# A fused attention and two-layer MoE kernel on one core: product 3 earlier in the second matmul, the next slice's x made later and for both halves at once, weight conversion in one half of the stage, and GpSimd's queue in emission order

## The chip, the cores and the metric

The kernel runs on one core of a Trainium2 chip (trn2). The metric is the device time of one execution in microseconds; lower is better. Engines are called by the names of the profile: PE (TensorE), PEld (its weight loads), DVE (VectorE), ACT (ScalarE), POOL (GpSimd) and SP (SyncE, which here only issues DMAs).

## What is computed

```python
def _attn_ref(q, k, v, g_norm):            # q, k, v: (8, 8, 576, 64)
    kv = np.einsum('bhsd,bhse->bhde', k, v)
    out = np.einsum('bhsd,bhde->bhse', q, kv)
    rms = np.sqrt(np.mean(out * out, axis=-1, keepdims=True) + 1e-06)
    return out / rms * g_norm

x = attn_out.transpose(0, 2, 1, 3).reshape(4608, 512)
h = x @ moe_w_in                           # 512 x 2048
x = (h / (1 + np.exp(-1.702 * h))) @ moe_w_out
h = x @ moe2_w_in
return (h - np.tanh(h)) @ moe2_w_out       # 4608 x 512
```

The weights arrive as 64-bit numbers and are converted on the chip.

## The kernel before

**Stages.** The 4608 tokens are cut into 8 slices of 576 (one batch each), and there are two layers, so the program runs 16 stages (l, n): layer l = 0 for n = 0 to 7, then layer l = 1. A stage has two halves. M1 (`m1`) multiplies x by the first weight matrix and applies the nonlinearity on ACT (L717); its results stand in the tiles `gt`. M2 (`m2`) multiplies these by the second weight matrix. The first slices use special code (`m1_plain`, `m2_plain`, `front_early`, `back_early`).

**Seven products.** Both halves replace the 8 block products of a 2 by 2 block multiplication by 7, numbered 1 to 7, whose operands are sums and differences of blocks. Each operand is split into a high and a low fp16 part, and three matmuls (high by high, high by low, low by high) stand for one in fp32. M2 takes its products in the order `ORDER2`, four steps each, 28 steps in all, 12 matmuls a step. A product accumulates in one pair of PSUM banks, X, Y or Z, halves d = 0 and d = 1. Products 1, 6, 7 and 4 share X, and each goes on adding to what the ones before left there, so PE may not start one before ACT has read the sum out (`scaled`, L839). What belongs to Y or Z is then added on DVE (`fma`, L833).

**The operands of M2.** For step i, DVE may first subtract one block of `gt` from another (`jA`, L771), ACT writes the high part (`jB`, L785) and DVE the low part (`jC`, L791) into one of seven buffers `jt`. The weights of M2 are streamed on SP's queue: 14 blocks `st` of 512 KB (`stream`, L812) through a ring of 4 buffers, one block for two steps. The weights of M1 stay on the chip (`wi`, 8 tiles).

**What runs beside.** Generators that are stepped at the end of every step (`tick`), at a rate for M1 and one for M2 (`add_side`), emit the side work. In stages (0, 2) to (0, 6) these are:

- `front(n + 1)` in M1: head products and numerators of the attention of the next slice. Its inputs come on POOL's queue, four units of keys and values of 640 KB (`xo<-atp`, L388) and two parts of queries of 576 KB (`scratch<-atp`, L388). It ends with the inverse roots, which are written to DRAM (`rd<-scratch`, L540).
- `back(n + 1)` in M2: the roots are read back, broadcast (`scratch<-rd`, L552, four of 288 KB), multiplied into the numerators (L653), and the seven operands of x are made by DVE subtractions (L344), ACT (L354) and DVE (L357). It ends with the fetch of the first inputs of the slice after.
- `conv1`: the second layer's 64-bit weights are loaded into `cbk` (L148, L149), turned into fp32 and split into fp16 by ACT and DVE (`words`, L160 to L166, and L175 to L181, L231), and written back to DRAM (`wid<-cbk`, L236; `wod<-cbk`, L239). All these DMAs are on POOL's queue.

In stage (0, 7) the first layer's `wi` are replaced by the second layer's: 8 reloads `wi<-wid` of 896 KB (L664) on POOL's queue. In layer 1 the side work is only loading x of the next slice (`scratch<-x2d`, L380, on SP's queue) and splitting it.

**What sets the order.** On PE and SP the instructions stand as they are emitted:

```python
man.enter_context(tc.manual_schedule(engines=frozenset([ENG.PE, ENG.SP])))
```

On the other engines a scheduler puts them in order from its own estimate of times. All engines run their own lists in order.

## Time and profile before

| | us |
|---|---|
| median of 3 runs | 1499.76 (1498.02 to 1500.09) |
| the profiled execution | 1500.06 |
| its span | 1498.3 |
| PE busy | 1431.6 (96%) |
| DVE busy | 1170.0 (78%) |
| ACT busy | 881.6 (59%) |
| POOL busy | 153.2 (10%) |
| DMA moved | 247.57 MB |

The profiled execution took 1.8 us more than its span, which runs from its first to its last instruction, and 0.3 us more than the median of the runs. A busy share is a mean over the stages, so the rows below are taken stage by stage.

### The profile page before, as it was taken

Reading aid. Unit: us, or ns where it says so; the run is one execution under the profiler, and the core shown is the slowest. Engines: PE = TensorE matmul, PEld = TensorE weight load, DVE = VectorE, ACT = ScalarE, POOL = GpSimd, SP = SyncE. Lnnn points to the kernel's source line nnn. Section 1 sums busy time; section 2 is a strip of 40 time slices with the busy share of each in tenths; the row PEclk is TensorE's granted clock in tenths of the full one; section 3 lists DMA queues with packets and bytes.
Section 4 is the critical chain, followed back from the end, with each engine's and each line's share of the span. In section 5 each row is a group of like instructions: output and inputs, shape, how many; then the busy total and the mean of one; then the engine's idle time right before and its main releaser. Section 6 shows DMA issues by size and latency. Waiting matters only on the chain.

```text
span 1498.3 us, 30084 instructions
## 1 busy us (share of the span) xinstructions
PE 1431.6 (96%) x11922; PEld 1108.8 (74%) x11922; DVE 1170.0 (78%) x2267; ACT 881.6 (59%) x1918; POOL 153.2 (10%) x238
## 2 busy tenths in 40 slices
PE   7999988999999899899989999999999999999998
PEld 5667756667777676677767777777777777777776
DVE  4998889587895776868879887868777787878485
ACT  5775554655756557567566555656464655555463
POOL 0001010121111202213031000000000000000000
PEclk9999999999999999999999999999999999999999
DMA  8776837267284582763788435160705243331504
GB/s 293 229 224 198 253 104 235 99 214 241 91 298 154 169 291 81 224 221 109 233 284 291 139 106 164 59 194 16 221 34 190 72 139 107 105 125 61 169 15 159
DMA packets 104686, 247.57 MB, mean 165 GB/s; under 512 B 10624, under 2 KB 55296, under 8 KB 104544
## 3 DMA queue, kind: packets, MB, share of 16 engines
q1 hardware_dynamic: 83504, 161.49, 33.4%
q0 software_dynamic: 21040, 84.15, 17.7%
q8 instruction: 93, 1.52, 0.4%
q14 instruction: 49, 0.40, 0.1%
HBM read 202.62 MB, written 42.98 MB: 164 GB/s over the span
## 4 chain that ended last, share of the span: by engine, by line
PE 71%; DVE 12%; DMA 8%; issue 5%; ACT 4%; SPq 0%; POOL 0%; DVEq 0%; POOLq 0%; ACTq 0%
PE X L896 7%; PE X L898 7%; PE X L897 7%; PE X L710 6%; PE X L712 6%; PE X L711 6%; PE Y L896 4%; PE Y L898 4%; PE Y L897 3%; DMA st<-wod 3%; PE Z L710 3%; PE Z L712 3%; PE Z L711 3%; DVE jt L791 2%; PE Z L896 2%
## 5 line engine op out<-in xcount | busy, mean ns | idle before, releaser
L785 ACT ACTIVATE jt<-gt 128x576 f16<-128x576 f32 x420 | 284.4, 682 | 180.3 <-PE X L898 63.8
L791 DVE SCALAR_TENSOR_TENSOR jt<-gt,jt 128x576 f16<-128x576 f32 x420 | 312.6, 754 | 74.7 <-ACT jt L785 71.3
L896 PE MATMUL X<-jt,st 128*128 128x288 f16 x960 | 274.5, 286 | 4.5 <-ACT gt L938 1.7
L897 PE MATMUL X<-jt,st 128*128 128x288 f16 x960 | 274.5, 286 | 2.9 <-DVE jt L791 2.9
L898 PE MATMUL X<-jt,st 128*128 128x288 f16 x960 | 274.5, 286 | 0.0
L710 PE MATMUL X<-xo,wi 128*128 128x288 f16 x896 | 256.4, 286 | 8.0 <-ACT mscratch L743 8.0
L712 PE MATMUL X<-xo,wi 128*128 128x288 f16 x896 | 256.2, 286 | 0.0
L711 PE MATMUL X<-xo,wi 128*128 128x288 f16 x896 | 256.2, 286 | 0.0
L896 PEld LDWEIGHTS <-st 128*128 128x128 f16 x1680 | 165.3, 98 | 64.3 <-DMA st<-wod 21.9
L898 PEld LDWEIGHTS <-st 128*128 128x128 f16 x1680 | 165.3, 98 | 49.4 <-issue 7.0
L897 PEld LDWEIGHTS <-st 128*128 128x128 f16 x1680 | 165.2, 98 | 49.0 <-issue 6.7
L710 PEld LDWEIGHTS <-wi 128*128 128x128 f16 x1568 | 153.3, 98 | 52.2 <-issue 13.4
L711 PEld LDWEIGHTS <-wi 128*128 128x128 f16 x1568 | 153.4, 98 | 48.6 <-issue 10.8
L712 PEld LDWEIGHTS <-wi 128*128 128x128 f16 x1568 | 153.4, 98 | 38.7
L771 DVE TENSOR_TENSOR gt<-gt 128x576 f32<-128x576 f32 x240 | 176.7, 751 | 1.6 <-ACT gt L717 1.2
L743 ACT COPY mscratch<-X 128x288 f32<-128x288 f32 x336 | 133.3, 397 | 75.5 <-PE X L712 69.1
L748 DVE TENSOR_TENSOR mscratch<-Z,mscratch 128x288 f32<-128x288 f32 x224 | 101.7, 454 | 75.1 <-PE Z L712 40.7
L896 PE MATMUL Y<-jt,st 128*128 128x288 f16 x480 | 137.3, 286 | 2.0 <-ACT gt L938 1.3
L897 PE MATMUL Y<-jt,st 128*128 128x288 f16 x480 | 137.3, 286 | 0.4 <-DVE jt L791 0.4
L898 PE MATMUL Y<-jt,st 128*128 128x288 f16 x480 | 137.3, 286 | 0.0
L710 PE MATMUL Z<-xo,wi 128*128 128x288 f16 x448 | 128.3, 286 | 0.4 <-DVE mscratch L748 0.4
L712 PE MATMUL Z<-xo,wi 128*128 128x288 f16 x448 | 128.1, 286 | 0.0
(249 smaller groups left out, 2505.2 us busy)
## 6 DMA issues: line engine op xcount, KB each, us to landing
st<-wod SPq DMA_DIRECT2D x210, 512.0 KB, 4.6
xo<-atp POOLq DMA_DIRECT2D x20, 640.0 KB, 6.2
scratch<-x2d SPq DMA_DIRECT2D x32, 288.0 KB, 6.0
cbk<-w_in POOLq DMA_DIRECT2D x32, 256.0 KB, 3.4
cbk<-w_out POOLq DMA_DIRECT2D x32, 256.0 KB, 5.0
scratch<-atp POOLq DMA_DIRECT2D x14, 576.0 KB, 6.3
scratch<-rd POOLq DMA_DIRECT2D x28, 288.0 KB, 8.8
x2d<-mscratch SPq DMA_DIRECT2D x28, 288.0 KB, 5.0
```

What stands on the lines that cost most here:

```text
L710: nc.tensor.matmul(out=out, lhsT=wh, rhs=xh, start=fresh and kt == 0, stop=False, skip_group_check=k)
L711: nc.tensor.matmul(out=out, lhsT=wh, rhs=xl, start=False, stop=False, skip_group_check=k)
L712: nc.tensor.matmul(out=out, lhsT=wl, rhs=xh, start=False, stop=kt == 1, skip_group_check=k)
L743: main(nc.scalar.copy(out=b.ap, in_=x))
L748: main(nc.vector.tensor_tensor(out=b.ap, in0=add[0], in1=b.ap, op=ALU.add))
L771: tt = lambda o, a, b: main(nc.vector.tensor_tensor(out=G[:, :, o, :], in0=G[:, :, a, :], in1=G[:, :, b, :], op=ALU.subtract))
L785: main(nc.scalar.activation(out=j[:, :, 0, :], in_=GT[STEPS2[i][1]][:, :, QD[STEPS2[i][0]], :], func=AF.Copy, scale=SX))
L791: main(nc.vector.scalar_tensor_tensor(out=j[:, :, 1, :], in0=GT[STEPS2[i][1]][:, :, QD[STEPS2[i][0]], :], scalar=SX, in1=j[:, :, 0, :], op ...
L896: nc.tensor.matmul(out=out, lhsT=wh, rhs=xh, start=a, stop=False, skip_group_check=k)
L897: nc.tensor.matmul(out=out, lhsT=wh, rhs=xl, start=False, stop=False, skip_group_check=k)
L898: nc.tensor.matmul(out=out, lhsT=wl, rhs=xh, start=False, stop=z, skip_group_check=k)
```

## The change

The new order of the products in M2 is 2, 1, 5, 3, 6, 7, 4; product 3 (on Y) stands between 5 and 6, and the sum of products 3 and 6 is finished after 6. In `back` the two halves of x are made together, three yields later, with one subtraction for both halves where there were two; its temporary moves to another region of the scratch tile. The next slice's inputs, all but the last unit, are fetched at its end. Conversion goes at rate 0.72 in M1 and 0 in M2 (before 0.64 and 0.2). POOL joins PE and SP in emission order. The reloads of `wi` go to SP and are emitted from M1 of stage (0, 7) on, and the conversion that must precede them is drained ahead of that M1. The rates of the early attention work in stages (0, 0) and (0, 1) change a little.

```diff
@@ -35,7 +35,7 @@
 WS = {4: 0, 1: 1, 2: 2, 5: 3, 6: 4, 3: 5, 7: 6}
 WO = {4: 0, 1: 1, 2: 2, 5: 4, 6: 5, 3: 6, 7: 7}
 TS = {1: 0, 7: 1, 2: 2, 3: 3, 5: 4, 6: 5, 4: 6}
-ORDER2 = (2, 1, 5, 6, 7, 3, 4)
+ORDER2 = (2, 1, 5, 3, 6, 7, 4)
 STEPS2 = ([(2, 0), (2, 1), (2, 2), (1, 0), (1, 1), (2, 3), (1, 2), (1, 3)] +
           [(r, i) for r in ORDER2[2:] for i in range(4)])
 FIRST2 = {r: min(i for i, s in enumerate(STEPS2) if s[0] == r) for r in ORDER2}
@@ -396,8 +396,18 @@
 
     def fetch(b):
 
-        ahead[b] = yield from unit_kv(b, 0)
-        ahead[b] = ahead[b], (yield from queries(b, 0))
+        kvs, qs = [(yield from unit_kv(b, 0))], []
+        yield
+        qs.append((yield from queries(b, 0)))
+        yield
+        if b > 2:
+            kvs.append((yield from unit_kv(b, 1)))
+            yield
+            qs.append((yield from queries(b, 1)))
+            yield
+            kvs.append((yield from unit_kv(b, 2)))
+            yield
+        ahead[b] = kvs, qs
 
     ahead = {}
     xbs, yt = {}, [None, None]
@@ -458,7 +468,7 @@
             yield from fetch(b)
             yield
             yield
-        kb, qb = ahead[b]
+        (kb,), (qb,) = ahead[b]
         for kt in range(2):
             for i in range(2):
                 head_products(i, kb.ap[:, 0:1280])
@@ -492,21 +502,20 @@
 
     def front(b):
 
-        kvs, qs = [ahead[b][0]], [ahead[b][1]]
-        kvs.append((yield from unit_kv(b, 1)))
-        qs.append((yield from queries(b, 1)))
+        kvs, qs = ahead[b]
+        xbs[b] = yield from rx.need(8 * H)
         for kt in range(2):
             for i in range(2):
                 kb = kvs.pop(0)
                 head_products(i, kb.ap[:, 0:1280])
                 kb.free()
-                if kt == 0:
-                    kvs.append((yield from unit_kv(b, 2 + i)))
+                if kt == i == 0:
+                    kvs.append((yield from unit_kv(b, 3)))
                 yield
             yield
-            xbs[b, kt] = yield from rx.need(4 * H)
             ex = yield from rs.need(4 * H)
-            og, sq = (t.ap.rearrange("p (i j n) -> p i j n", i=2, j=2) for t in (xbs[b, kt], ex))
+            og, sq = (t.rearrange("p (i j n) -> p i j n", i=2, j=2)
+                      for t in (xbs[b].ap[:, kt * 4 * H:(kt + 1) * 4 * H], ex.ap))
             qb = qs.pop(0)
             for j in range(2):
                 pair_numerators(qb.ap, j)
@@ -646,24 +655,53 @@
 
     def back(b, dst):
 
-        for _ in range(6):
-            yield
+        for _ in range(9):
+            yield
+        x = xbs[b].ap.rearrange("p (k n) -> p k n", k=2)
         for kt in range(2):
-            o, rb = xbs[b, kt].ap, rbs[b][kt]
-            nc.vector.scalar_tensor_tensor(out=o, in0=rb.ap, scalar=0.375 * SG, in1=o, op0=ALU.mult, op1=ALU.mult)
+            rb = rbs[b][kt]
+            nc.vector.scalar_tensor_tensor(out=x[:, kt], in0=rb.ap, scalar=0.375 * SG, in1=x[:, kt], op0=ALU.mult, op1=ALU.mult)
             rb.free()
             yield
-            ex = yield from rs.need(3 * H)
-            yield from xprep(xbs[b, kt], ex, dst[:, kt])
+        ex = yield from rq1.need(6 * H)
+        B = xbs[b].ap.rearrange("p (k s f) -> p k s f", k=2, s=4)
+        E = ex.ap.rearrange("p (k s f) -> p k s f", k=2, s=3)
+        tt = lambda o, a, b_: nc.vector.tensor_tensor(out=o, in0=a, in1=b_, op=ALU.subtract)
+        tt(E[:, :, 0, :], B[:, :, 1, :], B[:, :, 0, :])
+        yield
+        tt(B[:, :, 1, :], B[:, :, 3, :], B[:, :, 1, :])
+        yield
+        tt(E[:, :, 1, :], B[:, :, 3, :], E[:, :, 0, :])
+        yield
+        tt(E[:, :, 2, :], B[:, :, 2, :], E[:, :, 1, :])
+        yield
+        prev = None
+        for c in ((0, 2, B[:, :, 0:2, :]), (2, 4, B[:, :, 2:4, :]), (4, 6, E[:, :, 0:2, :]), (6, 7, E[:, :, 2:3, :]), None):
+            if c:
+                for kt in range(2):
+                    nc.scalar.activation(out=dst[:, kt, c[0]:c[1], 0, :], in_=c[2][:, kt], func=AF.Copy, scale=SX)
+            if prev:
+                a, z, src = prev
+                for kt in range(2):
+                    nc.vector.scalar_tensor_tensor(out=dst[:, kt, a:z, 1, :], in0=src[:, kt], scalar=SX,
+                                                   in1=dst[:, kt, a:z, 0, :], op0=ALU.mult, op1=ALU.subtract)
+            prev = c
+            yield
+        xbs[b].free()
+        ex.free()
         if b < NS - 1:
             yield from fetch(b + 1)
 
-    def reload():
-
-        for p in range(NP):
-            nc.gpsimd.dma_start(out=wi[p], in_=wid[p])
-            yield
-
+    def reload(p):
+
+        nc.sync.dma_start(out=wi[p], in_=wid[p])
+
+    def last_reload():
+
+        yield
+        yield
+        reload(NP - 1)
+        yield
 
     side, fixed = [], [False]
 
@@ -858,14 +896,12 @@
             elif r == 6:
                 o = scaled(x, d, 6)
                 fma(o, z, o)
+                fma(o, y, o)
+                quad(1, d, 6)
             elif r == 7:
                 o = scaled(x, d, 7)
                 fma(o, z, o)
                 quad(3, d, 7)
-            elif r == 3:
-                o = cc[6].ap[:, d * H:(d + 1) * H]
-                fma(o, y, o)
-                quad(1, d, 6)
             elif r == 4:
                 scaled(x, d, 4)
                 quad(2, d, 4)
@@ -1112,9 +1148,9 @@
             bk = fr = None
             if l == 0:
                 if n == 0:
-                    bk = add_side(both(1, xo[1]), 0.55, 1.0)
+                    bk = add_side(both(1, xo[1]), 0.58, 1.08)
                 elif n == 1:
-                    bk = add_side(both(2, xo[0]), 0.75, 0.85)
+                    bk = add_side(both(2, xo[0]), 0.78, 0.88)
                 elif n < NS - 1:
                     fr = add_side(front(n + 1), 0.56, 0.0)
                 else:
@@ -1123,11 +1159,15 @@
                 bk = add_side(x2load(n + 1, xo[(n + 1) % 2]), 0.4, 0.8)
             if (l, n) == (0, 2):
                 drain(dfr)
-                add_side(later, 0.64, 0.2)
+                add_side(later, 0.72, 0.0)
             if (l, n) == (0, 7):
                 rate(later, 0.64, 0.35)
+                while converted[0] < 16:
+                    next(later)
 
             def hook(p):
+                if (l, n) == (0, NS - 1) and p >= 2:
+                    reload(p - 2)
                 if p >= 2 and p % 2 == 0:
                     jcap[0] = (1, 2, 5)[p // 2 - 1]
                     jadvance(jcap[0])
@@ -1183,7 +1223,7 @@
                     fixed[0] = True
                     marks.clear()
                     marks.update({k: m for k, m in latest.items() if k == ENG.DVE})
-                man.enter_context(tc.manual_schedule(engines=frozenset([ENG.PE, ENG.SP])))
+                man.enter_context(tc.manual_schedule(engines=frozenset([ENG.PE, ENG.SP, ENG.Pool])))
                 tails = m1(l, n, hook)
             jcap[0] = 5
             if (l, n) == (1, 0):
@@ -1191,11 +1231,10 @@
             pre = [stream(l, i) for i in range(4)]
             if l == 0 and 1 < n < NS - 1:
                 drain([fr])
-                bk = add_side(back(n + 1, xo[(n + 1) % 2]), 0.0, 1.1)
+                bk = add_side(back(n + 1, xo[(n + 1) % 2]), 0.0, 1.0)
             if l == 0 and n == NS - 1:
-                while converted[0] < 16:
-                    next(later)
-                fr = add_side(reload(), 0.0, 0.4)
+                reload(NP - 2)
+                fr = add_side(last_reload(), 0.0, 1.0)
             m2(l, n, tails, pre)
             drain([bk, fr])
             man.close()
```

What moves is shown in three places. The first is POOL's list at the start of M2 of stage (0, 4). Before:

```order
L236 DMA wid<-cbk 128x1792
L540 DMA rd<-scratch 128x288
L388 DMA xo_71<-atp 128x1280
L148 DMA cbk<-w_in 128x2x256
L149 DMA cbk<-w_in 128x2x256
L552 DMA scratch<-rd 64x4x288 x4
L388 DMA xo_71<-atp 128x1280 x2
L388 DMA scratch<-atp 128x1152 x2
L236 DMA wid<-cbk 128x1792
```

Now (L549 is the write of the roots, L561 their broadcast):

```order
L549 DMA rd<-scratch 128x288
L561 DMA scratch<-rd 64x4x288 x4
L236 DMA wid<-cbk 128x1792
L148 DMA cbk<-w_in 128x2x256
L149 DMA cbk<-w_in 128x2x256
L388 DMA xo_71<-atp 128x1280
L388 DMA scratch<-atp 128x1152
L388 DMA xo_71<-atp 128x1280
L388 DMA scratch<-atp 128x1152
L388 DMA xo_71<-atp 128x1280 x2
```

The broadcasts moved ahead of the conversion's DMAs and of the keys and values; two of the three units that stood in this place moved behind the first part of the queries.

The second is ACT's list in M2 of the same stage, around the end of product 6. Before, where product 6 ends after step 15 (L839 reads X, L354 belongs to `back`, L785 is `jB`):

```order
L785 ACTIVATE jt<-gt_75 128x2x288
L785 ACTIVATE jt<-gt_76 128x2x288
L354 ACTIVATE xo_72<-scratch 128x2x288 x2
L785 ACTIVATE jt<-gt_73 128x2x288
L785 ACTIVATE jt<-gt_74 128x2x288
L839 ACTIVATE mscratch<-X_82 128x288
L839 ACTIVATE mscratch<-X_83 128x288
```

Now, where it ends after step 19 (L877 reads X, L682 belongs to `back`, L823 is `jB`; the first row is `jB` of step 22):

```order
L823 ACTIVATE jt<-gt_75 128x2x288
L682 ACTIVATE xo_72<-scratch 128x2x288 x4
L823 ACTIVATE jt<-gt_76 128x2x288
L682 ACTIVATE xo_72<-scratch 128x2x288
L823 ACTIVATE jt<-gt_73 128x2x288
L682 ACTIVATE xo_72<-scratch 128x2x288
L682 ACTIVATE xo_72<-scratch 128x288 x2
L823 ACTIVATE jt<-gt_74 128x2x288
L877 ACTIVATE mscratch<-X_82 128x288
L877 ACTIVATE mscratch<-X_83 128x288
```

The eight instructions of `back` that were spread over the M2 now stand in four places between `jB` of step 22 and the reading of X after product 6.

The third is SP's list in M1 of stage (0, 7). Before:

```order
L380 DMA scratch<-x2d 128x576 x4
L812 DMA st<-wod_92 128x2048 x4
L380 DMA scratch<-x2d 128x576 x4
L812 DMA st<-wod_92 128x2048 x5
```

Now (L697 is a reload):

```order
L697 DMA wi_63<-wid 128x3584
L697 DMA wi_64<-wid 128x3584
L380 DMA scratch<-x2d 128x576 x2
L697 DMA wi_65<-wid 128x3584
L380 DMA scratch<-x2d 128x576 x2
L697 DMA wi_66<-wid 128x3584
L697 DMA wi_67<-wid 128x3584
L697 DMA wi_68<-wid 128x3584
L850 DMA st<-wod_92 128x2048 x4
L697 DMA wi_69<-wid 128x3584
L380 DMA scratch<-x2d 128x576 x2
L850 DMA st<-wod_92 128x2048
```

Six of the eight reloads now stand ahead of the first four weight blocks of M2.

## Rows read from the trace of the kernel before

**Rows 1.** Windows by half stage: start:end, length, busy us (count), PEclk, DMA share, GB/s.

```profile
core 0: us, PE busy (x) PEld busy (x) DVE busy (x) ACT busy (x) POOL busy (x), PEclk, DMA share, GB/s
208.36:263.64 55.28, 43.99 (x344) 33.30 (x342) 51.01 (x86) 26.73 (x50) 6.91 (x12) 1.00 0.73 226
263.64:312.39 48.75, 47.32 (x448) 34.08 (x446) 31.62 (x68) 33.89 (x89) 6.49 (x10) 1.00 0.30 98
312.39:360.22 47.83, 44.39 (x350) 34.44 (x348) 40.90 (x75) 25.61 (x47) 7.75 (x13) 0.96 0.85 272
...
408.29:455.48 47.19, 44.57 (x351) 34.66 (x348) 41.99 (x76) 25.95 (x48) 8.45 (x14) 0.96 0.83 280
...
503.90:553.61 49.71, 44.81 (x350) 34.66 (x348) 40.12 (x71) 24.95 (x45) 9.69 (x16) 0.97 0.83 262
...
603.50:653.97 50.47, 44.90 (x351) 34.69 (x348) 43.54 (x79) 25.67 (x46) 11.69 (x18) 0.97 0.87 276
653.97:702.40 48.43, 47.82 (x454) 34.66 (x452) 31.83 (x68) 35.10 (x91) 10.97 (x15) 1.00 0.37 107
702.40:745.06 42.66, 42.66 (x350) 33.97 (x348) 41.65 (x76) 24.73 (x45) 7.42 (x11) 1.00 0.70 225
745.06:790.30 45.24, 40.38 (x326) 31.67 (x324) 33.78 (x73) 31.63 (x76) 12.79 (x19) 1.00 0.83 278
790.30:833.78 43.48, 42.81 (x350) 33.97 (x348) 40.09 (x73) 25.30 (x48) 8.01 (x11) 1.00 0.81 268
...
873.67:916.30 42.63, 42.63 (x350) 34.05 (x348) 33.76 (x59) 22.64 (x41) 2.14 (x3) 1.00 0.55 175
```

**Rows 2.** Waits of PE, whole span: us in total, times, longest.

```profile
PE Z L896 <- DMA st<-wod: 17.8, 8, 5.0
PE X L710 <- ACT mscratch L743: 8.0, 9, 2.5
...
PE X L896 <- ACT mscratch L839: 1.7, 2, 1.5
```

**Rows 3.** Windows again, 3.5 us in M2 of (0, 4).

```profile
526.30:529.80 3.50, 3.50 (x17) 2.24 (x16) 3.50 (x8) 2.65 (x5) 0.00 (x0) 0.51 0.98 388
```

**Rows 4.** DMA issues in 503.9:526, M2 of (0, 4): median us to landing.

```profile
st<-wod SPq DMA_DIRECT2D x5, 512.0 KB, 11.1
xo<-atp POOLq DMA_DIRECT2D x3, 640.0 KB, 16.4
scratch<-rd POOLq DMA_DIRECT2D x4, 288.0 KB, 12.5
cbk<-w_in POOLq DMA_DIRECT2D x2, 256.0 KB, 9.6
```

**Rows 5.** POOL's timeline, M2 of (0, 4): start, us, what [idle before].

```profile
511.64 1.10 POOL L388 DMA_DIRECT2D xo<-atp  x2
535.23 1.05 POOL L388 DMA_DIRECT2D scratch<-atp  x2 [22.49 <-DVE scratch L653]
```

**Rows 6.** DMA issues in 702.4:724.5, M2 of (0, 6).

```profile
st<-wod SPq DMA_DIRECT2D x6, 512.0 KB, 6.1
scratch<-rd POOLq DMA_DIRECT2D x4, 288.0 KB, 5.6
cbk<-w_out POOLq DMA_DIRECT2D x4, 256.0 KB, 5.2
```

**Rows 7.** DVE by line, M2 of (0, 4): busy us, mean ns, idle before.

```profile
L771 DVE TENSOR_TENSOR gt<-gt 128x576 f32<-128x576 f32 x10 | 7.3, 752 | 0.0
...
L653 DVE SCALAR_TENSOR_TENSOR scratch<-scratch 128x1152 f32<-128x1152 f32 x2 | 2.7, 1356 | 5.3 <-DMA scratch<-rd 5.3
```

**Rows 8.** ACT's timeline, M2 of (0, 6).

```profile
724.09 1.26 ACT L354 ACTIVATE xo<-scratch 128x576 f16<-128x576 f32 x2
```

**Rows 9.** ACT's timeline, M1 of (0, 7).

```profile
779.35 0.66 ACT L160 ACTIVATE cbk<-cbk 128x512 f32<-128x512 f32 x1 [4.40 <-DMA cbk<-w_out]
```

**Rows 10.** Who waited for tiles wi, M1 of (0, 7): us, times.

```profile
POOL wi L664: 20.8, 7
```

## The prediction

> **What bounds the kernel now.** I read the windows by half stage first, because a busy share over the span hides which stages lose time. The reader is to compare each length with PE's busy time in it. M2 of stage (0, 6) is 42.66 us long and PE is busy for all of it, as in M2 of (1, 0), 42.63: that is what an M2 costs when nothing stops it [rows 1]. M2 of (0, 2) to (0, 5) do the same arithmetic in 47.83, 47.19, 49.71 and 50.47 us, 195.2 in all, where four clean ones are 4 x 42.66 = 170.6. These four halves lose **24.6 us**. M2 of (0, 1) loses 12.6, with DVE busy for 51.0 of its 55.3. M1 of (0, 7) is 45.24 with PE busy for 40.38, a loss of 4.9, and M2 of (0, 7) loses 0.8 [rows 1].
>
> The waits of PE then say for what. By far the largest sum is for the weight blocks `st`, 17.8 us in 8 waits. The reading of X in M1 by ACT costs 8.0, the reading of X in M2 only 1.7 [rows 2]. A wait for `st` costs twice: in M2 of (0, 4) PE runs for 3.5 us after it at a granted clock of 0.51, the lower of its two levels (1.2 GHz), so that another 1.7 us go [rows 3]. The granted clock of the four halves is 0.96 or 0.97, that of (0, 6) 1.00 [rows 1].
>
> The DMA issues say why the blocks are late. In the first 22 us of M2 of (0, 4) a block takes 11.1 us to land, in (0, 6) 6.1 [rows 4, 6]. A step of M2 is 12 of the 350 matmuls, 1.46 us. The sixth block takes the ring's second buffer, which is free after step 5, and is needed at step 10: four steps, 5.9 us of room; the fifth has six, 8.8 us. So 6.1 just fits and 11.1 does not. What differs is POOL's load: in (0, 4) three units of keys and values (1,920 KB), two conversion loads (512) and four broadcasts (1,152), in (0, 6) four conversion loads (1,024) and the broadcasts [rows 4, 6], each with one write of the conversion and one of the roots beside. That is 3.6 against 2.2 MB. Two of the units were issued at 511.64, 7.7 us into the M2, long before they were wanted [rows 5].
>
> **The change, part by part** (T is the start of an M2, in which step k begins at about T + 1.7 + 1.46 k).
>
> *POOL in emission order.* In this stretch stand now the broadcasts, two conversion loads and one unit: 1,152 + 512 + 640 = 2.3 MB, close to (0, 6). Between 2.2 MB (6.1 us) and 3.6 MB (11.1 us) this gives 6.1 + 0.1/1.4 x 5.0 = 6.5 us, 0.6 over the room of one block. Bounds: no wait, as in (0, 6), and half of the present loss, if one unit and the broadcasts together are already too much. I take 0.4 us a half, since the load is nearest to (0, 6). The other units wait behind the first queries, whose buffer `back` now frees near its end, about T + 34.5. Before, the first queries were issued 31 us into this M2, when DVE freed their buffer [rows 5]. Queries and the next unit, 1.2 MB at about 270 GB/s [rows 1], are there at T + 40, and PE wants that unit some 3 us into the next M1, T + 47: I cost this at nothing.
>
> *x made later and for both halves at once.* Before, DVE stood for 5.3 us in M2 of (0, 4) for the broadcasts [rows 7]; with the multiplication behind step 14, about T + 18, they have landed. As many elements are subtracted in half the instructions, which I cost at nothing: DVE is not what ends these halves (40 to 44 us busy in 47 to 50, and the conversion leaves M2) [rows 1]. What it costs is on ACT. The order puts eight instructions of `back` and three `jB` between `jB` of step 22 and the reading of X behind product 6. The first of them need the second difference. From about T + 17.7, when I take the low part for step 14 to be done, three steps ahead of its use, DVE does two multiplications (2.7 us), six low parts and two differences at 0.75 [rows 7], 8.7 in all: T + 26.4. Then ACT has six copies of full width at 0.63 [rows 8], two of half width, taken at 0.4, and three `jB` of full width, at 0.6: 6.4 us, T + 32.8 for the reading to begin if each follows the last. Product 7 adds to X and stands at step 20, T + 30.9. So PE waits, about **1.5 us** with some overlap between ACT's instructions, in each of (0, 2) to (0, 6). Bounds: 0 (DVE earlier by two steps) and 3.5 with a drop of the clock. The order that puts 7 behind 6 and 4 behind 7 leaves no product of another bank between them.
>
> *Sum for M2.* Four halves of 42.66 + 0.4 + 1.5 = 44.56 make 178.2, **-17.0**. M2 of (0, 6) had no wait and gets one: **+1.5**.
>
> *Conversion at 0.72 in M1, none in M2.* One eighth more in M1 of (0, 2) to (0, 6). DVE is busy for about 32 us of 48 there, ACT for 34 or 35 [rows 1], so it fits between; but ACT must read X at every few steps, and the 8.0 us for it [rows 2] can grow, while the units that came early before cost less bandwidth now. The first and the last of these five lost 1.4 and 0.6 (length less PE busy) [rows 1]. I take **+1** for the five; bounds -3 (all of the loss) and +5 (1 each).
>
> *Stage (0, 7).* Before, POOL's reloads stood waiting for PE for 20.8 us [rows 10], the conversion's loads behind them came late, and ACT stood for 4.4 us in one conversion step while PE wanted X [rows 9]. With the reloads on SP that wait should go, and I take back 3.7 of the 4.9 of M1. But on SP the reloads stand ahead of the first weight blocks of M2. Reload 5 can go when PE is done with its tile, some 8 us before T, and the blocks only after it: 0.9 + 2.0 MB at 278 GB/s [rows 1] are 10.4 us. The first block lands before T, the fourth at about T + 2.5, which is wanted at step 6; yet reload 6 and the conversion run beside. I take +2.7 for M2, together **-1**. Bounds: -5 (both losses gone) and +7.
>
> *The rest.* M2 of (0, 1) is bound by DVE and its order hardly moves: -0.5, bounds -3 and +3. The first matmuls of the next M1 stand ahead of the last 42 of M2 and need product 7's sum read from Z on DVE; before, product 7 was over four steps earlier. Estimated from the same step times they want it at T + 37.5 and it is there at about T + 37.3. I add **+0.8** for 14 stages with so little room and for one more conversion item ahead of layer 1; bounds 0 and +8.
>
> **Sum:** -17.0 + 1.5 + 1 - 1 - 0.5 + 0.8 = -15.2 on the profiled execution's 1500.06: **1485**. The median lies 0.3 lower, which I leave out.
>
> **The rivals.**
>
> *A. The weight blocks of (0, 7) come behind the reloads.* The four blocks on SP that were asked for together early in this M1 had time; now the reloads ahead of them hold up SP itself. For: SP's order, and 20.8 us of such waits on POOL [rows 10]. Against: 8 us of room. If each of the first blocks is late, M2 loses 8 us more: 1493.
>
> *B. The denser conversion stops M1.* ACT reads X late by 2.5 us (the longest now [rows 2]) in each of the five halves, 12.5 in place of 1: 1496.5. For: ACT is the busiest after PE there. Against: a quarter of its time is free.
>
> *C. The burst stays.* The broadcasts, two conversion loads and a unit are still in one stretch, and the order on POOL's queue alone does not bring `st` forward. Half of the 24.6 us stays, 12.3 in place of 1.6: 1495.7. For: the broadcasts themselves took 12.5 us under load [rows 4]. Against: they took 5.6 in (0, 6) [rows 6], with nearly the same load. The Trainium skill, "DMA: Bandwidth & Descriptors", section "Queues, rings and completion order", says that each DMA engine goes round between the queues that have work, packet by packet; by that rule it would not matter to a block what stands in POOL's queue, only for how long something does. The trace of before agrees as far as 11.1 against 6.1 us goes. The same page, section "Issuing engines are not separate DMA queues", says that another issuing engine saves little but issue time; by it the reloads' move would bring nothing in bandwidth, and only the end of POOL's waits counts.
>
> *D. Slower: product 7's sum is read too late.* From (0, 2) on, the first six matmuls of the next M1, which write Z, stand ahead of the last 42 of M2 in PE's list. Before, two products followed 7, now one. If ACT's and DVE's reading of 7 is done 1.5 us after PE wants Z, PE stands 1.5 us in each of 14 stages: 21 in place of 0.8, and the time is 1505. It decides from about 1.3 us late (14 x 1.3 = 18, the gain and 3 more). For: my estimate leaves 0.2 us, and in (0, 2) to (0, 6) everything behind ACT's eight instructions slips. Against: in layer 1 little stands in front of that reading, DVE is busy for 33.8 of 42.6 us in M2 of (1, 0) [rows 1].
>
> **How the numbers follow.** Forecast 0.56 (1475 to 1489), A 0.14, B 0.10, C 0.10, D 0.07, and 0.03 for more than the forecast's gain: no wait for ACT in M2 and both losses of (0, 7) gone (under 1474). The range from 1474 to 1497 leaves out D, that last case and the upper halves of B and C, together 0.19. A difference under 0.2%, 3 us, can't be told from none for this kernel. Faster than 1496.8: the forecast, the last case, nearly all of A and somewhat over half of B and C, 0.83. Within 0.2%: 0.08. Slower than 1502.8: D and the tails of the others, 0.09.
>
> **What would show it.** Right: no or hardly a wait of PE for `st` and a granted clock of 1.00 in M2 of (0, 2) to (0, 5); lengths near 44.6; in all five M2, (0, 6) too, a wait of PE for the reading of X by ACT of about 1.5 us behind product 6; ACT no longer standing for 4 us in M1 of (0, 7). Wrong: waits for `st` in M2 of (0, 7) (A), longer M1 of (0, 2) to (0, 6) with waits for ACT (B), waits for `st` as before (C), PE's first matmuls of M1 on Z waiting for DVE in layer 1 (D), and, against the term at nothing, its head products waiting for `xo<-atp`.

## The result, and the profile after

The changed kernel takes **1488.38 us** (median of 5 runs, 1481.82 to 1491.17) where the kernel before takes 1499.76 (1498.02 to 1501.78). The ratio is 0.9917 with a 95% interval of 0.989 to 0.9943: faster by 0.6 to 1.1%. The forecast was 1485, in a range of 1474 to 1497. The profiled execution took 1489.31 us, 10.75 less than that of before, and its span is 1487.5.

The windows of the changed kernel by half stage, cut as in [rows 1]: M1 of (0, 2), M2 of (0, 2), (0, 4), (0, 5), (0, 6), then M1 and M2 of (0, 7). In the changed kernel, from (0, 2) on, the first six matmuls of the next M1 (0.74 us) stand inside each M2; in the kernel before, and with the old order of products, they stand behind it. So that much must be taken off an M2 of the changed kernel and added to the M1 behind it before a comparison.

```profile
core 0: us, PE busy (x) PEld busy (x) DVE busy (x) ACT busy (x) POOL busy (x), PEclk, DMA share, GB/s
...
263.39:314.58 51.19, 48.14 (x454) 34.66 (x452) 33.54 (x73) 34.76 (x91) 9.29 (x14) 1.00 0.35 115
314.58:359.88 45.30, 43.87 (x357) 34.54 (x354) 38.89 (x66) 23.81 (x43) 7.65 (x13) 1.00 0.80 259
...
501.30:548.27 46.97, 43.85 (x356) 34.54 (x354) 39.29 (x67) 23.84 (x44) 7.65 (x13) 1.00 0.77 253
596.23:641.93 45.70, 43.86 (x356) 34.54 (x354) 39.26 (x67) 24.42 (x44) 8.61 (x14) 1.00 0.78 257
689.93:734.77 44.84, 43.68 (x356) 34.63 (x354) 38.98 (x67) 24.46 (x45) 5.96 (x9) 1.00 0.63 202
734.77:780.75 45.98, 41.28 (x320) 31.75 (x318) 36.79 (x76) 31.51 (x77) 10.96 (x15) 0.96 0.79 258
780.75:825.25 44.50, 43.71 (x354) 34.57 (x355) 38.63 (x72) 25.92 (x48) 6.73 (x10) 1.00 0.81 290
```

M2 of (0, 3) is 45.30 as well. So the four M2 that lost 24.6 us come to 183.27, less 4 x 0.74, 180.3: 14.9 less than before. The granted clock in them is 1.00 where it was 0.96 or 0.97. But M1 of (0, 2) got 2.4 longer, M2 of (0, 6) 1.4, and M1 of (0, 7) is no shorter. The table sets the terms of the forecast beside what the two profiles show.

| place | forecast | measured |
|---|---|---|
| M2 of (0, 2) to (0, 5) | -17.0 | -14.9 |
| M2 of (0, 6) | +1.5 | +1.4 |
| M1 of (0, 2) to (0, 6) | +1 | +2.7, of it (0, 2) +2.4 |
| stage (0, 7) | -1 | +1.8 (M1 +1.5, M2 +0.3) |
| M2 of (0, 1) | -0.5 | +0.1 |
| layer 1 | +0.8 | -1.5 |
| start, rounding | | -0.4 |
| sum | -15.2 | -10.8 |

The waits of PE over the whole span of the changed kernel:

```profile
PE X L932 <- ACT mscratch L877: 8.5, 7, 3.0
PE X L748 <- ACT mscratch L781: 8.3, 11, 2.7
...
PE Z L932 <- DMA st<-wod: 3.1, 4, 2.0
```

The wait for weight blocks fell from 17.8 to 3.1 us [rows 2]. The reading of X in M2 grew from 1.7 to 8.5: 1.0 in each M2 of (0, 2) to (0, 6), 3.5 in (0, 1). The DMA issues of the first 22 us of M2 of (0, 4), and POOL's timeline there, to be read against [rows 4, 5]:

```profile
st<-wod SPq DMA_DIRECT2D x5, 512.0 KB, 7.4
scratch<-rd POOLq DMA_DIRECT2D x4, 288.0 KB, 7.8
xo<-atp POOLq DMA_DIRECT2D x1, 640.0 KB, 8.3
cbk<-w_in POOLq DMA_DIRECT2D x2, 256.0 KB, 6.7
```

```profile
505.81 2.46 POOL L561 DMA_DIRECT2D scratch<-rd  x4 [2.01 <-PE Y L934]
508.27 0.57 POOL L236 DMA_DIRECT2D wid<-cbk  x1
517.35 0.71 POOL L148 DMA_DIRECT2D cbk<-w_in  x1 [8.51 <-DMA wid<-cbk]
...
518.77 0.55 POOL L388 DMA_DIRECT2D xo<-atp  x1
537.08 0.55 POOL L388 DMA_DIRECT2D scratch<-atp  x1 [17.76 <-DVE xo L686]
537.62 0.53 POOL L388 DMA_DIRECT2D xo<-atp  x1
```

The four broadcasts go first. The conversion's loads wait for its write to land, 8.5 us, and the unit of keys and values behind them is issued 17.5 us into the M2; the rest follows at 537, 36 us in. A block lands in 7.4 us where it took 11.1 (5.9 to 6.7 in M2 of (0, 2), (0, 3) and (0, 5), where it took 8.4 to 10.8).

Three places on ACT's timeline carry the losses: M1 of (0, 2), M2 of (0, 4) and M1 of (0, 7).

```profile
274.05 0.66 ACT L160 ACTIVATE cbk<-cbk 128x512 f32<-128x512 f32 x1 [3.00 <-DMA cbk<-w_in]
...
529.51 2.39 ACT L682 ACTIVATE xo<-scratch 128x576 f16<-128x576 f32 x4
...
535.34 0.68 ACT L877 ACTIVATE mscratch<-X 128x288 f32<-128x288 f32 x2
...
763.07 0.66 ACT L160 ACTIVATE cbk<-cbk 128x512 f32<-128x512 f32 x1 [3.81 <-DMA cbk<-w_out]
```

At 274 ACT stands for the conversion's first load, which on POOL's list is now behind a unit that waits for PE. At 529 to 535 the eight instructions of `back` delay the reading of product 6. At 763 ACT stands for a conversion load as it did before [rows 9].

### The profile page after: what moved, and what is told of

The parts are those of the page before. It is cut to its first block, busy times and chain, and to the rows that moved or that the text cites. A ratio compares the mean times of both kernels' runs of the same rounds, so it can differ in the third digit from the quotient of the medians.

```text
span 1487.5 us, 30033 instructions
## 1 busy us (share of the span) xinstructions
PE 1429.6 (96%) x11922; PEld 1109.4 (75%) x11922; DVE 1164.3 (78%) x2247; ACT 880.3 (59%) x1918; POOL 147.8 (10%) x230
## 4 chain that ended last, share of the span: by engine, by line
PE 65%; DVE 16%; DMA 8%; issue 5%; ACT 5%; POOL 0%; SPq 0%; DVEq 0%; ACTq 0%; POOLq 0%
PE X L748 6%; PE X L750 6%; PE X L749 6%; PE X L932 5%; PE X L933 5%; PE X L934 5%; PE Y L932 3%; DVE jt L829 3%; PE Y L934 3%; PE Y L933 3%; PE Z L748 3%; PE Z L749 3%; PE Z L750 3%; DMA st<-wod 2%; DMA x2d<-mscratch 2%
## 5 line engine op out<-in xcount | busy, mean ns | idle before, releaser
L823 ACT ACTIVATE jt<-gt 128x576 f16<-128x576 f32 x420 | 285.2, 683 | 186.8 <-PE Y L934 41.4
```

What stands on the lines that cost most here:

```text
L823: main(nc.scalar.activation(out=j[:, :, 0, :], in_=GT[STEPS2[i][1]][:, :, QD[STEPS2[i][0]], :], func=AF.Copy, scale=SX))
```

## The experiments

Twelve runs were made, in three groups of four, each group on one chip beside the kernel before. The stretch in the table runs from the first matmul of M2 of (0, 2) to that of M2 of (0, 6), by the profile: 390.0 us before, 375.4 in the changed kernel and 372.4 in its second profile.

| run | median, us | before in the group | ratio, 95% interval | stretch, us |
|---|---|---|---|---|
| pool_by_scheduler | 1508.25 | 1499.51 | 1.006 (1.0044 to 1.0076) | 397.5 |
| old_product_order | 1501.57 | 1499.51 | 1.0013 (0.9999 to 1.0026) | 387.3 |
| slow_conversion_stage_7 | 1489.12 | 1499.51 | 0.9929 (0.9915 to 0.9944) | 377.4 |
| first_load_early | 1490.25 | 1499.51 | 0.9937 (0.9923 to 0.9951) | 376.9 |
| three_between_6_and_7 | 1486.46 | 1501.28 | 0.9907 (0.9884 to 0.9929) | 371.1 |
| old_order_8_buffers | 1483.63 | 1501.28 | 0.9884 (0.9862 to 0.9907) | 369.0 |
| reload_on_pool | 1489.88 | 1501.28 | 0.9926 (0.9902 to 0.9949) | 373.1 |
| change_again | 1491.27 | 1501.28 | 0.9936 (0.9911 to 0.9961) | 372.4 |
| change_8_buffers | 1490.31 | 1499.72 | 0.994 (0.9925 to 0.9955) | 371.4 |
| conversion_as_before | 1506.56 | 1499.72 | 1.0048 (1.0032 to 1.0064) | 392.8 |
| three_late_8_buffers_more | 1486.34 | 1499.72 | 0.9914 (0.9896 to 0.9932) | 375.9 |
| three_middle_8_buffers_more | 1484.31 | 1499.72 | 0.9898 (0.988 to 0.9915) | 373.8 |

### POOL's list

```diff
-man.enter_context(tc.manual_schedule(engines=frozenset([ENG.PE, ENG.SP, ENG.Pool])))
+man.enter_context(tc.manual_schedule(engines=frozenset([ENG.PE, ENG.SP])))
```

> The changed kernel, but POOL's list is left to the scheduler again; so the broadcasts stand behind the conversion's write, one unit of keys and values and two conversion loads, and two more units stand right behind them, as before the change. Theory: POOL's list is what shortened M2 of (0, 2) to (0, 5). Then waits of PE for weight blocks come back there, 2 to 4 us a half with the low clock behind the longer ones, the four halves grow by 8 to 15 us in sum, and M1 of (0, 2) gets back the 2.4 us that it lost to the late first conversion loads: 1494 to 1501. Rival: the halves are shorter because the conversion left M2 and x is made later; then POOL's list makes under 3 us, M1 of (0, 2) still gains 2.4, and the time is 1484 to 1489.

Measured: 1508.25, slower than before the change. M2 of (0, 2) to (0, 5) are 52.56, 51.43, 51.72 and 51.48 us long, 24 more in sum than in the changed kernel; M1 of (0, 2) is 48.18, 3.0 less. PE's waits in M2 of (0, 2) to M1 of (0, 6), and the DMA issues of the first 22 us of M2 of (0, 4):

```profile
PE Z L932 <- DMA st<-wod: 19.2, 5, 5.1
PE X L932 <- ACT mscratch L877: 4.0, 4, 1.0
```

```profile
st<-wod SPq DMA_DIRECT2D x5, 512.0 KB, 10.9
xo<-atp POOLq DMA_DIRECT2D x3, 640.0 KB, 14.5
```

Three units stand in this stretch again, a block lands in 10.9 us, and the waits for blocks are back; the wait for ACT stays. The theory holds, and the effect is larger than expected: beside the other parts, POOL's list is worth 17 to 20 us (1508.25 against 1491.27 and 1488.38), more than the whole change. Without it the rest of the change makes the kernel slower.

### The place of product 3, and the buffers for sums and copies

```diff
-ORDER2 = (2, 1, 5, 3, 6, 7, 4)
+ORDER2 = (2, 1, 5, 6, 7, 3, 4)
```

With it, `fin` adds product 3 in a branch of its own, as before the change.

> The changed kernel with the products of M2 in the old order 2, 1, 5, 6, 7, 3, 4. ACT's eight instructions of back then stand behind the reading of product 6 and ahead of that of product 7, behind which product 3, on Y, runs. Theory: the wait of PE of 1.0 us for ACT's reading of X in each M2 of (0, 2) to (0, 6) comes from product 3 no longer standing between two products on X; it goes, M2 of (0, 6) is 42.7 to 43.1, and the time is about 5 us shorter, 1482 to 1485. Rival: the order was changed because DVE or ACT need the room elsewhere, and the same microsecond is lost at another place, as a wait for jt or for the sum of product 7: 1487 to 1491.

Measured: 1501.57, 10 to 13 us slower than the changed kernel. The wait for ACT in M2 is gone as the theory said, and M2 of (0, 2) to (0, 6) are 43.1 to 45.0. But M1 of (0, 3) to (0, 6) are 54.10, 49.34, 55.00 and 53.67 us. The rival is right that the time is lost elsewhere, at a place and of a size that neither named. PE's and ACT's waits of the stretch, ACT's timeline at the start of M1 of (0, 3), and the DMA issues of 350 to 362 us:

```profile
PE X L748 <- ACT mscratch L781: 14.8, 9, 4.7
PE Z L934 <- DMA st<-wod: 2.2, 2, 1.7
...
ACT mscratch L781 <- DMA x2d<-mscratch: 17.8, 3, 6.3
```

```profile
365.31 0.40 ACT L781 COPY mscratch<-X 128x288 f32<-128x288 f32 x1 [5.38 <-DMA x2d<-mscratch]
```

```profile
xo<-atp POOLq DMA_DIRECT2D x3, 640.0 KB, 8.6
scratch<-atp POOLq DMA_DIRECT2D x2, 576.0 KB, 8.2
x2d<-mscratch SPq DMA_DIRECT2D x3, 288.0 KB, 10.6
```

ACT's copy of X needs a buffer in `mscratch`, and the next ones in turn were held by a result of M2 until its store had landed. The fetch at the end of `back` now puts four transfers, 2.4 MB, on the DMA engines just ahead of these stores, from 35.2 us into M2 of (0, 2) on, and a store takes 10.6 us. At the end of M2 of (0, 4) before the change, with no fetch there, it took 5.2:

```profile
x2d<-mscratch SPq DMA_DIRECT2D x2, 288.0 KB, 5.2
```

In the changed kernel stores are about as slow at this place (10.0). What differs is the turn. The class `Scratch` of the kernel hands out the seven in a ring: in M1 of (0, 3), (0, 5) and (0, 6) the first copy gets a buffer of the sum of product 6, in (0, 4) the second copy does. With the old order this sum waits for product 3 and is the second of two stores, out 38.8 us into M2 of (0, 2) and landed at 49.94; the copy begins at 49.96. In the changed kernel it is the first of the two, out at 38.1 and landed at 47.38; the copy begins at 47.40. Besides, M1 of (0, 3) begins 1.0 us earlier with the old order, so its copy waits for longer. M1 of (0, 4), where the first copy finds a free buffer, is the one of 49.34 us. So the new order pays for the moved fetch. Two runs test this. The first gives the old order one buffer more, and nothing else:

```diff
-SCRATCH, MAIN = 5896, 7 * 288
+SCRATCH, MAIN = 5896, 8 * 288
```

> The run with the old order of the products, and the tile that holds sums and copies (mscratch) larger by one buffer of 128 x 288, 8 in place of 7. Theory: M1 of (0, 3) to (0, 6) stood for 4 to 5 us because ACT's first copies of X found no free buffer until a store of M2 had landed. One more lets one copy go, so this wait falls by 1.5 us or more in each of the four: 1492 to 1497 where the old order alone has 1501.6. Rival: no buffer was lacking and the wait is for something else that ends then: within 2 us of the old order, 1500 to 1503.

Measured: **1483.63**, 18 us less than the old order with seven. PE's and ACT's waits of the stretch:

```profile
PE X L748 <- ACT mscratch L781: 1.9, 5, 0.4
PE Z L934 <- DMA st<-wod: 1.7, 3, 1.1
...
ACT mscratch L781 <- DMA x2d<-mscratch: 4.3, 4, 1.3
```

PE's 14.8 became 1.9, and ACT's waits for a store fell from 17.8 us to 4.3. The theory holds, with more effect than expected: the low clock behind each long wait goes too. The granted clock of M1 of (0, 3), (0, 5) and (0, 6) was 0.97, 0.94 and 0.97 with seven buffers and is 1.00 with eight. The second run puts 3 between 6 and 7; `fin` adds product 3 to the sum of 6 in a branch of its own again:

```diff
-ORDER2 = (2, 1, 5, 3, 6, 7, 4)
+ORDER2 = (2, 1, 5, 6, 3, 7, 4)
...
                 fma(o, z, o)
+            elif r == 3:
+                o = cc[6].ap[:, d * H:(d + 1) * H]
                 fma(o, y, o)
                 quad(1, d, 6)
```

> The changed kernel with the products of M2 in the order 2, 1, 5, 6, 3, 7, 4. Theory, after the run with the old order: two things decide the place of product 3. Between two products on X it saves PE the 1.0 us at ACT's eight instructions; and it must be over four steps before the end, so that the sum of 3 and 6 is stored and its buffer free before M1 of the next stage wants it, since the fetch at the end of back makes these stores land after 10 us. This order has both: no wait for ACT behind product 6, M2 of (0, 2) to (0, 6) at 43.4 to 44.5 (the first six matmuls of M1 in it) where the changed kernel has 44.8 to 47.0, M1 of (0, 3) to (0, 6) at 47 to 48.5: 1481 to 1485. Rival: the wait of the old order came from the order itself (the reading of 7 behind ACT's eight instructions, as late here as there), M1 of (0, 3) to (0, 6) grows to 50 or more, and the time is 1490 to 1502.

Measured: 1486.46, on one chip with 1491.27 for the changed kernel; the intervals of the two overlap, so the traces must tell. M2 of (0, 2) to (0, 6) are 43.4 to 44.2, with no wait for ACT's reading in the stretch; M1 of (0, 3) to (0, 6) are 48.4 to 49.4, a little over what was expected. The sum of 3 and 6 is stored at 35.5 us in M2 of (0, 2) to (0, 4), just ahead of the fetch, and lands in 5 to 7. The theory holds: one microsecond a half is the price of two products on X in a row, and with seven buffers the sum of 3 and 6 must be the first of the late stores.

> The changed kernel, with 8 buffers in place of 7 in the tile of sums and copies. Theory: with product 3 early the stores are early too and a buffer is seldom lacking (ACT stood 3 us in all for stores in its profiles), so 7 suffice for that order: 0 to 2 us shorter than the changed kernel on the same chip, the wait of 1.0 for ACT in each M2 stays, 1486 to 1491. Rival: lacking buffers cost the changed kernel as well, in waits that the profile puts down to something else; then it comes down to the 1484 of the old order with 8.

The same line on `MAIN` in the changed kernel: 1490.31 (0.994 of the kernel before on its chip, where the changed kernel has 0.9917 and 0.9936) and a stretch of 371.4, against 375.4 and 372.4. No difference that can be told, as the theory said: with the new order seven buffers are enough.

### The conversion

```diff
-add_side(later, 0.72, 0.0)
+add_side(later, 0.64, 0.2)
```

> The changed kernel with the conversion at 0.64 in M1 and 0.2 in M2 as before the change. Theory: the conversion's 6 us of DVE in M2 of (0, 2) to (0, 6) make x later, ACT's eight instructions and the reading of product 6 behind them too, and its DMAs stand in the stretch in which the weight blocks are late; M2 grows by 0.5 to 2 us each, M1 of (0, 2) to (0, 6) falls by under 0.5 each: 1490 to 1498. Rival: DVE and DMA have the room in M2 and M1 is the tighter half; then it is 1486 to 1490 with the waits for X in M1 shorter.

Measured: 1506.56, 15 to 18 us slower than the changed kernel, and beyond what the theory expected, at another place. M2 of (0, 2) to (0, 5) are no longer than in the changed kernel (44.3 to 45.5); M1 of (0, 3) to (0, 6) are 51.9 to 55.3. ACT's waits from 316 to 710 us:

```profile
ACT mscratch L781 <- DMA x2d<-mscratch: 22.1, 6, 6.0
```

It is the lack of buffers again, though the order is the new one. With conversion work on DVE in M2, the sum of 3 and 6 goes to its store 39.8 to 40.3 us into M2 of (0, 2) to (0, 5), where the second profile of the changed kernel has 38.1 to 38.4, and lands at 49.6 to 52.9 for 46.3 to 47.9. Part of this can be the fetch: in M2 of (0, 2) it starts 38.6 us into the half (POOL stood for DVE's conversion, L178), 34.5 in the changed kernel, and then lies on the last stores, which take 9.7 to 13.0 us. But in M2 of (0, 4) it starts at 35.2, no later than in the changed kernel (34.7 and 35.8), and M1 behind it is 52.90 us long as well. So ACT's row shows the wait for stores, and the times that the sum is stored later. The share of the fetch is not shown: no run moved it alone, and none gave this kernel an eighth buffer.

The first load of the conversion was moved ahead, by one step of its generator in front of M1 of (0, 2):

```diff
                 drain(dfr)
+                next(later)
                 add_side(later, 0.72, 0.0)
```

> The changed kernel with the conversion's first load emitted ahead of M1 of (0, 2), so that on POOL's list it stands ahead of the keys and values that wait there for PE until 2.7 us into the M1. Theory: ACT's 3.0 us for this load in M1 of (0, 2), and with it the two waits of PE of 1.0 and 1.5 us, come from this place on the list; M1 of (0, 2) falls from 51.2 to 48.5 to 49.3, the rest stays: 1485 to 1487. Rival: the conversion at the higher rate needs what M1 of (0, 2) hasn't got, and the waits move to a later item there: 51 as now, 1487 to 1490.

M1 of (0, 2) fell from 51.19 to 48.00, more than expected, and ACT no longer stands there: the place on POOL's list was the cause. But the time is 1490.25. Part of it, in this profile, is M2 of (0, 1), 60.0 for 55.0 to 57.0 in the others of the new order with seven buffers. The scheduler puts the early load there (POOL issues it at 237 us), but the two last runs, which have it too, take 56.8 and 55.1. And M1 of (0, 5) and (0, 6) got longer, 49.46 and 50.32 for 47.96 and 48.00. The rival, that the wait only moves, stands: not to a later item of this half, but to later halves.

### Stage (0, 7)

```diff
-                rate(later, 0.64, 0.35)
+                rate(later, 0.4, 0.65)
```

> The changed kernel with the conversion in stage (0, 7) at rate 0.4 in M1 and 0.65 in M2 in place of 0.64 and 0.35. Theory: M1 of (0, 7) did not get shorter because the conversion's own chain (write lands, load is issued, load lands, ACT) is slower than its rate beside 0.9 MB reloads, whichever queue holds these; with fewer items in M1 the waits of ACT for conversion loads go, M1 of (0, 7) falls from 46.7 to 42 or 43 and M2 grows by less than 1: 1483 to 1486. Rival: the waits move to M2 with the items, and the two halves together stay within 1.5 us of the changed kernel's 90.5: 1487 to 1490.

M1 of (0, 7) fell to 40.89, but M1 of (1, 0), up to the end of which what is left of the conversion has to be emitted, grew from 38.96 to 41.10. The two halves of (0, 7) and M1 of (1, 0) together take 126.7, against 129.4 in the first profile of the changed kernel and 126.8 in its second: nothing that can be told, and 1489.12 says the same.

```diff
-        nc.sync.dma_start(out=wi[p], in_=wid[p])
+        nc.gpsimd.dma_start(out=wi[p], in_=wid[p])
```

> The changed kernel with the 8 reloads of wi in the same place of the program but on POOL's queue in place of SP's. Theory: what matters is the bytes beside the conversion; but on POOL's list a reload that waits for PE also holds up the conversion's loads and writes behind it, so M1 of (0, 7) gets 1 to 4 us longer than the changed kernel's 46.0, and M2 of (0, 7), with its weight blocks free on SP, up to 1 shorter: 1488 to 1492. Rival: on SP the reloads held up the weight blocks and the loads of x, and POOL is the better place: 1484 to 1487.

Neither came about as worded: M1 of (0, 7) is 43.06, shorter by 2.9, and M2 47.41, longer by 2.9. The sum is 90.47 against 90.48 in the first profile of the changed kernel (its second has 87.8), and the time 1489.88 against 1491.27 in the same group, intervals overlapping. The second profile of the changed kernel has 43.59 for this M1, so only the 2.9 in M2 stand out (44.2 there). A gain or loss in the whole by the queue that holds the reloads can't be told.

> The changed kernel as it is, once more on this chip, to see what differs from one profile to the next with nothing changed: 1482 to 1491, and by half stage within 1 us of the first profile except where weight blocks land late in M2 of (0, 1) to (0, 5), where I expect up to 4 us either way.

1491.27, and in the second profile M1 of (0, 7) is 43.59 where the first had 45.98, M2 of (0, 4) 44.98 for 46.97, M2 of (0, 1) 56.70 for 55.37. The first of these was not among the halves for which more than 1 us was expected. Differences of 2 us in these halves are no finding in one profile.

### All together

> The old order of the products with 8 buffers (1483.6 before), and two things more: the conversion's first load ahead of M1 of (0, 2), and its rates in (0, 7) 0.45 and 0.7. Theory: M1 of (0, 2) falls by 1.5 to 2.5 us as in the run with the first load early, the halves of (0, 7) and M1 of (1, 0) by 0 to 3 together: 1479 to 1483. Rival: both only move waits to the next half, 1483 to 1486.

> The same two things and 8 buffers with the order 2, 1, 5, 6, 3, 7, 4. Theory: with 8 buffers the place of product 3 matters only in that it stands between two products on X; then this equals the run beside it within 2 us: 1479 to 1484. Rival: an earlier store of the sum of 3 and 6 still pays, 1475 to 1479, or the reading of product 7 behind ACT's eight instructions costs, 1484 to 1488.

Measured: 1486.34 and 1484.31. Their ratios to the kernel before, 0.9914 and 0.9898, lie below the two of the change (0.9917 and 0.9936), but the intervals overlap. Neither beats the old order with 8 buffers alone (0.9884), whose interval they overlap too. The rates of (0, 7) shortened M1 of (0, 7) to 40.52 and 40.29. In the first run this went into M1 of (1, 0), 44.33 us with a wait of 2.8 for ACT, where the old order with 8 buffers alone has 39.89; in the second it stayed. The early first load is the likely cause of what was lost elsewhere, as these halves grew in the run with it alone too: M1 of (0, 5) is 52.65 and 52.43, M1 of (0, 6) 51.00 and 51.28, where the old order with 8 buffers alone has 48.38 and 48.20. POOL's timeline in M1 of (0, 5) of the second run:

```profile
543.66 0.53 POOL L388 DMA_DIRECT2D xo<-atp  x1 [8.17 <-PE AT L443]
544.18 0.55 POOL L236 DMA_DIRECT2D wid<-cbk  x1
553.62 0.72 POOL L148 DMA_DIRECT2D cbk<-w_out  x1 [8.89 <-DMA wid<-cbk]
```

One item earlier, a write of the conversion stands behind the unit that waits 8.2 us for PE, and the next load behind its landing. A queue in emission order keeps every such neighbourhood, good and bad.

## Why the prediction was right, and where not

**The burst at the start of M2: right, and the largest part.** The step read the loss from the blocks' landing against the room in the ring, and expected 6.5 us by the bytes on POOL's queue; 7.4 were measured in M2 of (0, 4) and 5.9 to 6.7 in the three others, and 2.8 us of waits for blocks in the stretch where I had summed 1.6. Leaving POOL's list to the scheduler brought 10.9 us and the waits back. Rival C, half the burst staying, did not happen: POOL's work was spread, the unit coming at 17.5 us. That fits the rule of the Trainium skill named there ("DMA: Bandwidth & Descriptors", "Queues, rings and completion order"), by which each DMA engine goes round between the queues that have work. No run changed the order in the stretch and kept its bytes, so it is not shown apart from their amount.

**ACT's eight instructions: right in place, a third less than forecast.** 1.0 us in each of five halves, forecast 1.5. In M2 of (0, 4) the first copies began at 529.51, 28.2 us into the half, 26.2 without the 2.0 us that PE had stood for a block before (forecast 26.4 for the second difference); the reading began at 535.34, in the same count 32.0 where 32.8 had been summed. M2 of (0, 6) came out at +1.4 for +1.5. Three between 6 and 7 takes the wait away, so its cause is shown.

**Conversion in M1: mis-sized, and its use not seen.** I gave +1 for five halves and named conversion in M1 as a price. It cost +2.7, nearly all in (0, 2) and not by its rate: POOL's list put the first load behind a waiting unit. What the step missed is that taking the conversion out of M2 is worth 15 to 18 us here, by the traces because the sum of 3 and 6 is stored 1.5 to 2.2 us earlier.

**The fetch at nothing: right by luck.** The step asked only whether the units come in time for PE, and they did; no wait of PE for `xo<-atp` appears. It did not ask what 2.4 MB at the end of M2 do to the stores beside them, which went from about 5 to 10 us. In the changed kernel that costs little (ACT stood 3.1 us in all for stores), because the sum of 3 and 6 is stored first and the conversion is out of the way. Take back either, and 10 to 18 us are lost. The prediction had no term for the reason for which the new order is worth its place.

**Stage (0, 7): the step that failed.** "With the reloads on SP that wait should go, and I take back 3.7 of the 4.9 of M1." M1 got 1.5 longer, and 0.9 shorter in the second profile. POOL's wait for PE did go, but another took its place. POOL's waits in this M1, before and now:

```profile
POOL wi L664 <- PE Z L712: 12.5, 5, 4.3
POOL wi L664 <- PE Y L712: 6.9, 1, 6.9
POOL cbk L148 <- DMA wod<-cbk: 4.3, 2, 2.2
...
POOL cbk L148 <- DMA wod<-cbk: 21.1, 4, 7.5
```

POOL issues a conversion load only after the write before it has landed, in 5 to 6 us by the median, and the load takes 5.4 more. Before, most of that landing passed while POOL stood for PE. So ACT's waits for conversion loads only fell from 6.0 to 5.1 us (the longest 3.8), and PE's waits for X from 4.7 to 4.1. What made M1 longer is the clock: behind the longest of these waits, 2.7 us, PE ran 5 us at a granted clock of 0.68, where it kept 1.00 before.

```profile
765.00:770.00 5.00, 5.00 (x30) 3.47 (x29) 3.59 (x10) 2.29 (x6) 1.42 (x2) 0.68 0.42 111
```

By these figures that costs an estimated 1.6 us (5 x 0.32). In the second profile the longest wait is 2.1 us and the clock stayed at 1.00. The other term of the stage, +2.7 for M2, failed as well: +0.3, and 0.0 in the second profile. There the stage comes to -0.9 for the -1 of the forecast, by two errors that cancel. The Trainium skill, "DMA: Bandwidth & Descriptors", section "Issuing engines are not separate DMA queues", cited in the prediction under rival C, says that issuing from another engine saves little but issue time. The run with the reloads on POOL agrees: 90.47 us for the two halves against 90.48 and 87.8. Rival A itself did not happen: 0.6 us of wait for the first block.

**Layer 1: the sign was wrong.** +0.8 was set for the narrow room at the next M1's first matmuls, and rival D rested on it; no wait of PE for Z appears there, and layer 1 took 1.5 less. Some 0.8 of that is the wait for a weight block in the last M2, 1.2 us before and 0.4 now.

The sum came out at -10.8 for -15.2: 2.1 short in the four M2, 2.8 in (0, 7), 1.7 in M1, less 2.3 gained in layer 1. Of the 9.7 us that the four M2 still lose, the waits for ACT are 4.0 (forecast 6.0) and those for blocks 2.8 (1.6). The other 2.9, of which 0.6 are waits for DVE, stand under no term of the sum, and their cause stays open: the two terms together were not too small, but the 42.66 under them was not reached.

## What to carry to other kernels

When a burst of transfers is moved, price it twice: what it leaves (the loads that were late) and what it lands on, stores included, and ask which buffers those stores hold and who takes one next. A change of several parts can hang together: here any one of three parts undone alone brings the kernel back to its old time or above it, and one more buffer of 1152 bytes a partition did what the new order of products does, and better: 1483.6 for 1491.3 on one chip. When a wait is to be taken away, ask what else runs out during it: in stage (0, 7) POOL's wait for PE had hidden the landing of a write. And whether the reloads sat on SP's queue or POOL's gave no gain that could be told.

## What the runs showed that I had not expected

Two profiles of one program differ by up to 2.4 us in a half that depends on DMA (M1 of (0, 7), 45.98 at a granted clock of 0.96 and 43.59 at 1.00), so a term of that size needs a median or a second profile. And the length of a wait does not tell alone what becomes of the clock: in the last run a wait of 2.7 us in M1 of (0, 6) left the granted clock of that half at 1.00, one of 2.2 in M1 of (0, 5) left 0.97; in the changed kernel 2.7 us in M1 of (0, 7) left 0.96. I would price a wait of 2 to 3 us with a range that holds both.
